# The first stage of a spectral layer and a gated feed-forward network, dealt out anew over the engines of one core

## The chip, the core and the metric

The kernel runs on one core of a Trainium2 chip. The core has engines with a queue of their own each: PE (TensorE, matmuls; its weight loads are listed as PEld), DVE (VectorE), ACT (ScalarE), POOL (GpSimd) and SP (SyncE, which here only issues transfers). Transfers are carried by 16 DMA engines. An engine works through its instructions in program order and waits on semaphores for what others produce. The metric is the device time of one execution in microseconds (us).

## The reference

`x` has 2048 rows of 576 elements (bf16). A global spectral filter is added to it, then a gated feed-forward network with 4608 hidden columns:

```
X = rfft2(layernorm(x))               # over rows and columns, 2048 x 289
y = irfft2(X * (w_r + 1j * w_i))      # bf16
h = x + y
n = layernorm(h)
out = h + (gelu(n @ w_gate) * (n @ w_up)) @ w_down
```

## The kernel before

The whole transform is done with matmuls against tables of sines and cosines that the kernel makes itself. `h_sb` holds the 2048 rows as 16 groups of 128 (one row group h is `h_sb[:, h, :]`). The order of every engine's instructions is that of the program text: `tc.manual_schedule()` is set, so nothing is moved by a planner.

**First stage.** Constants are written by DVE (`zerob` and others, L78 to L87). POOL writes the index ramps (`iota`, L173, called from L181 on) and the identity matrix; DVE makes from them the angles `mu` (L202), the mask (L212), `s2p` and `ks` (L217, L219). The row statistics of `x` come in two ways: even groups, and 13 and 15, by DVE (`sd`, which calls `ln_dve`, L117 to L119, three instructions), the other odd ones by ACT (`ln_act`, L124, two passes with a sum each, completed on POOL by `ln_fin`, L128 and L129). POOL turns variances into reciprocal roots four or two groups at a time (`ln_rstd`, L133 and L134, the second a power). `norms(lo, hi)` normalises groups on DVE (`xn`, L137) and calls `row16(h)` for each: PE multiplies the group by the row table `F16` (L306; remainder columns by `row16_rest`, L319). `fill` (L294) issues matmuls whose result nobody reads: 16 before the first group, 1 before each of groups 1 to 11, 5 behind the last. ACT brings the products from PSUM to `Bt` (`evict`, L330, and `evict4`, L336; the last `evict4` is DVE's).

Beside it tables are made. `DT` holds the column sines: the turns `kd` (`turns`, L271 and L272), the phases `pd` (`phases`, L276) and an operation that drops the sign (`drop_sign`, L225) on DVE, then two passes on ACT (`col_sin`, L355). `DF`, `DI` and `DS` hold shifted parts of `DT`: `DF` by two DVE copies (L414, L415), `DI` by one transfer and one DVE copy (L444), `DS` by four transfers (`sine_rows`, L431). `TF` holds the twiddle factors, 9 slices: angles on DVE (`angle_a`, L238 and L246; `angle_b`, L249 and L225), `sine` and `cosine` on ACT (L253, L256), `minus_sine` on DVE (L259), and `turn_tf` (L262), a transposing transfer to `TI`. Two slices (`first`) are made at the start and seven (`rest`) later. The spectral weights `WR` and `WI` come by transfers (L154), their far rows through two indirect transfers issued by POOL (L376, `wm_r` and `wm_i`) and one DVE operation each (L434, L436); two short DVE operations halve the edge columns (L438).

All PSUM tiles of this part come from one ring of four buffers (`two`, L66), so a product can start only when the tile four allocations back has been evicted.

**Second stage.** The loop from L651 on runs over eight pairs of row frequencies (`order`). For each pair: `f2` (L483, six matmuls with `Bt` against `DT` and `DF`; evicted to `pq` by ACT, one of them by DVE, L491), `f3` (L498, L499, twiddle matmuls with `TF`; evicted by ACT, L519), `sums_of` (L528, L529, DVE), `wmul` (L546 to L558, the spectral weights on DVE; the sums of the next pair are made in its middle), `i3` (L574, L576, matmuls with `TI`). In its first rounds the loop also makes the `rest` of the twiddles and calls `late_tables` (L444 to L456: the `DI` copy, four matmuls into `pt`, two ACT passes to `G16`).

**Third part.** Column products back (`inv_cols`, L623), the sum with `x` (`add_rows`, `add_sum`), the second layer norm, and the feed-forward network: 4 blocks of 512 rows, 36 hidden tiles each (`gu`, L881), then `acc` (L901). Its weights come in groups of three tiles (`load_gu`, L145, two transfers of 432 KB); the first three groups are called for at L155, ahead of the first stage's work, and `wd_a` (1728 KB) behind `turn_tf(rest)`. SP issues all transfers but POOL's two, in program order.

Of the kernel before, what the change touches and what calls it, by code (L numbers as in the profile page):

```python
# [10 lines left out]
ALU = mybir.AluOpType  # L11
# [30 lines left out]
def kernel_body(  # L42
# [129 lines left out]
    def iota(t, pattern, base=0, cm=0):  # L172
        G.iota(t, pattern=pattern, base=base, channel_multiplier=cm, allow_small_or_imprecise_dtypes=True)  # L173
# [23 lines left out]
    iota(iJ[:], [[1, 2], [2, JH]])  # L197
    rev = tmp("rev", [P, 1])
    iota(rev[:], [[0, 1]], 2 * P - 1, -2)

# [9 lines left out]
    V.tensor_scalar(iu[:], iu[:], 7, None, op0=ALU.bitwise_and)  # L210
    mask = tmp("mask", [P, P], FP32)
    V.tensor_scalar(mask[:], iu[:].rearrange("p c l -> p (c l)"), 0.0, None, op0=ALU.is_equal)  # L212
# [8 lines left out]
    iDs = tmp("iDs", [P, 3], FP32)  # L221
# [26 lines left out]
    def angle_b(sl):  # L248
# [12 lines left out]
    def turn_tf(sl):  # L261
        nc.sync.dma_start(  # L262
            TI[:, sl].rearrange("p k r q -> p (k r) q"), TF[:, sl].rearrange("p k r q -> p (k r q)"), transpose=True
        )

    pd, kd = tmp("pd", [P, 3, JP], FP32), tmp("kd", [P, 3, JP], FP32)
    C23 = 8388608.0

    def turns():
        for t in range(3):  # L270
            V.tensor_scalar(kd[:, t, :], iJ[:], iDs[:, t : t + 1], C23, op0=ALU.mult, op1=ALU.add)  # L271
        V.tensor_scalar(kd[:], kd[:], -C23, -float(D), op0=ALU.add, op1=ALU.mult)  # L272

    def phases():
        for t in range(3):
# [20 lines left out]
    def row16(h):  # L296
        if h % 2 == 0 or h == H - 1:
            ps_f[h] = two("f2t")
        if h % 4 == 0:
            ps_f["f4", h] = two("f4")  # L300
        f2t, b = (ps_f[h], 0) if h in ps_f else (ps_f[h - 1], 1)
        fill(f2t[:, b, :], 16 if h == 0 else 1 if h < 12 else 0)
        x = xn[:, h, :]
        for t in range(2):
            for n, d0 in ((0, t * P), (1, DH + t * P)):
                T.matmul(  # L306
                    f2t[:, b, t * 2 * P : (t + 1) * 2 * P],
                    lhsT=x[:, d0 : d0 + P],
                    rhs=F16[:, n : n + 2, :],
                    start=(n == 0),  # L310
                    stop=(n == 1),
                )
        if h < 12:
            row16_rest(h)
# [46 lines left out]
        )  # L361

    first, rest = slice(0, 2), slice(2, 9)
    angle_a(first)
    angle_b(first)
    ln_act(1)
    ln_act(3)
    sine(first)
    cosine(first)
    sd(0)  # L370
    row_table()
    sd(2)
# [2 lines left out]
    for t, w in zip(wm, (A_w_r, A_w_i)):  # L375
# [6 lines left out]
    turns()  # L382
    minus_sine(first)
    turn_tf(first)
    ln_act(5)
    ln_act(7)
    norms(0, 4)
    sd(4, 6)
    ln_fin(slice(5, 8, 2))
    ln_rstd(rstd, mv, 4, 8)  # L390
    evict(0, 2)
    evict4(0)
    ln_act(9)
    phases()
    norms(4, 8)
    drop_sign(kd[:], pd[:])
    ln_act(11)
    evict(4, 6)
    evict4(4)
    col_sin(1, pd, zerob)  # L400
    sd(8, 10)
    ln_fin(slice(9, 12, 2))
    ln_rstd(rstd, mv, 8, 12)
    sd(12, 13)
    ln_rstd(rstd, mv, 12, 14)
    norms(8, 12)
    sd(14, 15)
    ln_rstd(rstd, mv, 14, 16)
    evict(8)
    col_sin(0, kd, hpib)  # L410
    evict(10)
    evict4(8)
    norms(12, 16)
    V.tensor_copy(DF[0:32], D3[0:32])  # L414
    V.tensor_copy(DF[96:128], D3[96:128])  # L415
    for h in range(12, 16):
        row16_rest(h)
    evict(12, 14, 15)
    fill(two("f2t")[:, 0, :], 5)

    def sine_rows():


        for dst, src in (
            (DI[64:128, :, 1, :], DT[0:64, 0, :, 1, :]),
            (DS[0:64, 0, :, :], DT[64:128, 0, :, 1, :]),
            (DS[64:128, 0, :, :], DT[0:64, 1, :, 1, :]),
            (DS[0:64, 1, :, :], DT[64:128, 1, :, 1, :]),
            (DS[64:128, 1, :, :], D3[0:64, :, 1, :]),
        ):  # L430
            nc.sync.dma_start(dst, src)  # L431

    def weights():
        V.tensor_copy(WR[:, 9 : H + 1, 0:J], wm[0][:].rearrange("p (r j) -> p r j", r=8))  # L434
        evict4(12)
# [4 lines left out]
    weights()  # L440
    sine_rows()

    def late_tables():
        V.tensor_copy(DI[0 : J - 2 * P, :, 0, :], D3[0 : J - 2 * P, :, 0, :])  # L444
        pt = two("pt")
        for x in range(2):
            for p0 in (0, 64):
                T.matmul(
                    pt[p0 : p0 + 64, 0, x * P : (x + 1) * P],
                    lhsT=F16[:, 0, 64 * x : 64 * x + 64],  # L450
                    rhs=ident[:],
                    start=True,
                    stop=True,
                )
        for sign in range(2):
            A.activation(  # L456
                G16[:, sign, :, :].rearrange("p x q -> p (x q)"),
                pt[:, 0, 0 : 2 * P],
                ACT.Copy,
                scale=G_SCALE if sign == 0 else -G_SCALE,  # L460
            )

    xn_pool.__exit__(None, None, None)
    spw = tc.tile_pool(name="spw", bufs=1)
# [13 lines left out]
    def f2(c):  # L478
        ps = two("pq_ps")
        col = slice(slot[c] * P, (slot[c] + 1) * P)  # L480
        for par in range(2):
            for t in (par, par + 2, 4):
                T.matmul(  # L483
                    ps[:, par, 0:JP],
                    lhsT=Bt[:, t, col],
                    rhs=DT[:, t // 2, par] if t < 4 else DF[:, par],
                    start=(t == par),
                    stop=(t == 4),
                )
        sb = wk.tile([P, 2, JP], BF16, name="pq", tag="pq", bufs=6)  # L490
        (V.tensor_copy if c == 9 else A.copy)(  # L491
            sb[:].rearrange("p r (j a) -> p r j a", a=2),
            ps[:, :, 0:JP].rearrange("p a (r j) -> p r j a", r=2),
        )
        pq[c] = sb
# [156 lines left out]
    for i in range(n + 1):  # L652
# [12 lines left out]
        if 1 <= i <= n:  # L665
            f3(order[i - 1], 1)
            if i == 1:
                sums_of(order[0])
                sine(rest)
                angle_b(rest)  # L670
            else:
                if i == 2:
                    cosine(rest)
                    minus_sine(rest)
                    turn_tf(rest)
                    nc.sync.dma_start(wd_a[:], wd_view[:, 0:NWA, :])
                wmul(order[i - 2], i - 1, order[i - 1])
        if i >= 3 and not last:
# [288 lines left out]
```

## Time and profile before

| what | value |
|---|---|
| median of 3 runs | 508.18 us (508.09 to 509.54) |
| the profiled execution | 508.19 us, span 506.4 us |
| granted clock of PE | 0.999 |

Busy time of each engine by stretch, from the table of windows of the trace:

| stretch, us | what runs there | PE | DVE | ACT | POOL | DMA GB/s |
|---|---|---|---|---|---|---|
| 0 to 10.6 | tables, first statistics | 4.99 | 8.93 | 7.80 | 4.36 | 292 |
| 10.6 to 29.0 | row products | 14.84 | 16.94 | 13.76 | 8.03 | 243 |
| 29.0 to 35.7 | first `f2`, `f3` | 6.34 | 5.55 | 4.93 | 0 | 58 |
| 35.7 to 63.8 | `wmul` of all pairs | 27.00 | 27.61 | 26.09 | 0 | 89 |
| 63.8 to 78.0 | back, sum, second norm | 13.30 | 9.24 | 11.41 | 2.14 | 173 |
| 78.0 to 506.4 | feed-forward network | 424.83 | 147.29 | 87.19 | 9.63 | 112 |

The span runs from the first instruction to the last; the time of an execution has 1.8 us more around it. In lines of the timeline the first two numbers are start and duration in us, then come the engine, the line of the kernel, the operation, the tile written and the tiles read with their shapes, the count, and in brackets how long the engine had been idle and who released it. In the chain of waits a line is one piece of the path that ended last: start, length, engine, tile, line. Instructions of one engine overlap a little, so a duration can reach past the next start.

### The profile page before, as it was taken

Reading aid. Unit: us, or ns where it says so; the run is one execution under the profiler, and the core shown is the slowest. Engines: PE = TensorE matmul, PEld = TensorE weight load, DVE = VectorE, ACT = ScalarE, POOL = GpSimd, SP = SyncE. Lnnn points to the kernel's source line nnn. Section 1 sums busy time; section 2 is a strip of 40 time slices with the busy share of each in tenths; the row PEclk is TensorE's granted clock in tenths of the full one; section 3 lists DMA queues with packets and bytes.
Section 4 is the critical chain, followed back from the end, with each engine's and each line's share of the span. In section 5 each row is a group of like instructions: output and inputs, shape, how many; then the busy total and the mean of one; then the engine's idle time right before and its main releaser. Section 6 shows DMA issues by size and latency. Waiting matters only on the chain.

```text
span 506.4 us, 9895 instructions
## 1 busy us (share of the span) xinstructions
PE 491.3 (97%) x4342; PEld 291.2 (57%) x4342; DVE 215.6 (43%) x436; ACT 151.2 (30%) x265; POOL 24.2 (5%) x64
## 2 busy tenths in 40 slices
PE   5799999999999999999999999999999999999997
PEld 2466775555557764444477744444577544444775
DVE  8989964789651015533310034333201233333001
ACT  6888984222330003232300023333200132323000
POOL 4400010111110000000000000000000000000000
PEclk9999999999999999999999999999999999999999
DMA  9977068779970019997720089987500588880000
GB/s 293 247 89 195 1 167 215 148 147 195 185 143 1 0 48 191 187 201 151 154 57 0 1 187 197 186 166 151 100 0 1 119 163 155 160 153 3 12 13 25
DMA packets 86988, 60.86 MB, mean 120 GB/s; under 512 B 22688, under 2 KB 85536, under 8 KB 86944
## 3 DMA queue, kind: packets, MB, share of 16 engines
q1 hardware_dynamic: 86656, 59.03, 59.2%
q0 software_dynamic: 288, 1.18, 0.8%
q8 instruction: 34, 0.56, 0.5%
q14 instruction: 10, 0.08, 0.1%
HBM read 52.65 MB, written 2.36 MB: 109 GB/s over the span
## 4 chain that ended last, share of the span: by engine, by line
PE 91%; DVE 5%; DMA 1%; ACT 1%; POOL 1%; issue 0%; POOLq 0%; DVEq 0%
PE gu L881 55%; PE acc L901 28%; PE pq_ps L483 2%; DMA wd<-in_B_w_down_dram 1%; PE cs_ps L623 1%; PE eo_ps L576 1%; PE f2t L306 1%; PE eo_ps L574 1%; DVE xn L137 1%; PE gh_ps L499 1%; ACT cwb L636 1%; DVE st L118 1%; PE y_ps L746 1%; DVE st L117 1%; PE gh_ps L498 1%; POOL rstd L134 0%
## 5 line engine op out<-in xcount | busy, mean ns | idle before, releaser
L881 PE MATMUL gu<-Bt,wgu 64*128 64x512 bf16 x2592 | 281.5, 376 | 0.8 <-ACT cwb L636 0.8
L881 PEld LDWEIGHTS <-wgu 64*128 64x128 bf16 x2592 | 131.2, 94 | 147.9 <-issue 1.8
L889 ACT ACTIVATE g_sb<-gu 128x512 f32<-128x512 f32 x144 | 86.0, 597 | 302.7 <-PE gu L881 302.7
L890 DVE TENSOR_TENSOR P_sb<-g_sb,gu 128x512 bf16<-128x512 f32 x144 | 98.7, 685 | 152.8 <-ACT g_sb L889 152.8
L901 PEld LDWEIGHTS <-P_sb 128*128 128x128 bf16 x1152 | 112.4, 98 | 30.6 <-issue 2.4
L901 PE MATMUL acc<-wd,P_sb 128*128 128x288 bf16 x768 | 99.3, 286 | 0.0
L913 DVE TENSOR_TENSOR h_sb<-h_sb,acc 128x576 bf16<-128x576 bf16 x15 | 11.3, 754 | 118.2 <-PE acc L901 118.2
L901 PE MATMUL acc<-wd_a,P_sb 128*128 128x288 bf16 x384 | 52.3, 286 | 0.5 <-DVE h_sb L909 0.5
L294 PE MATMUL f2t<-h_sb,ident 128*128 128x512 bf16 x32 | 10.5, 434 | 4.4 <-DMA h_sb<-in_A_x_dram 4.4
L306 PE MATMUL f2t<-F,xn 128*128 128x256 bf16 x64 | 9.3, 273 | 4.8 <-DVE xn L137 4.8
L483 PE MATMUL pq_ps<-DT,Bt 128*128 128x290 bf16 x64 | 12.4, 287 | 0.0
L771 DVE TENSOR_SCALAR hrow<-h_sb,mv,rstd 128x1152 bf16<-128x1152 bf16 x14 | 12.1, 867 | 0.0
L134 POOL TENSOR_TENSOR rstd<-rstd,mhalf 128x1 f32<-128x1 f32 (+2 forms) x17 | 11.8, 692 | 1.4
L623 PEld LDWEIGHTS <-EO 128*128 128x128 bf16 x96 | 9.1, 96 | 3.0 <-issue 0.2
L483 PEld LDWEIGHTS <-Bt 128*128 128x128 bf16 x96 | 9.2, 97 | 2.5 <-ACT Bt L330 0.2
L491 ACT CAST pq<-pq_ps 128x580 bf16<-128x580 f32 x15 | 9.8, 667 | 1.9 <-PE pq_ps L483 1.9
L306 PEld LDWEIGHTS <-xn 128*128 128x128 bf16 x64 | 5.9, 98 | 7.7 <-DVE xn L137 6.1
L118 DVE BATCH_NORM_STATS2 st<-h_sb 128x6 f32<-128x288 bf16 x22 | 9.7, 442 | 0.0
L117 DVE BATCH_NORM_STATS2 st<-h_sb 128x6 f32<-128x288 bf16 x22 | 9.7, 442 | 0.0
L133 POOL TENSOR_SCALAR rstd<-mv 128x1 f32<-128x1 f32 (+2 forms) x17 | 4.3, 251 | 112.6 <-DVE mv L119 112.6
L330 ACT CAST Bt<-f2t 128x1024 bf16<-128x1024 f32 (+1 forms) x9 | 8.1, 927 | 5.0 <-PE f2t L306 5.0
L498 PE MATMUL gh_ps<-pq,TF 128*128 128x289 bf16 x32 | 8.7, 286 | 0.6 <-ACT TF L256 0.6
(134 smaller groups left out, 250.5 us busy)
## 6 DMA issues: line engine op xcount, KB each, us to landing
wgu<-in_B_w_gate_dram SPq DMA_DIRECT2D x48, 432.0 KB, 5.3
wgu<-in_B_w_up_dram SPq DMA_DIRECT2D x48, 432.0 KB, 6.7
wd<-in_B_w_down_dram SPq DMA_DIRECT2D x2, 1728.0 KB, 8.3
wd_a<-in_B_w_down_dram SPq DMA_DIRECT2D x1, 1728.0 KB, 8.4
out_dram<-h_sb SPq DMA_DIRECT2D x3, 576.0 KB, 3.3
h_sb<-in_A_x_dram SPq DMA_DIRECT2D x4, 288.0 KB, 3.3
h_sb<-in_A_x_dram SPq DMA_DIRECT2D x2, 576.0 KB, 5.6
WR<-in_A_w_r_dram SPq DMA_DIRECT2D x1, 650.2 KB, 7.8
```

The costliest lines, as they stand in the source:

```text
L117: V.bn_stats(st[:, 0, :], h_sb[:, h, 0:DH])
L118: V.bn_stats(st[:, 1, :], h_sb[:, h, DH:D])
L134: G.tensor_tensor(dst[:, sl], dst[:, sl], mhalf[:, sl], ALU.pow)
L306: T.matmul(f2t[:, b, t * 2 * P : (t + 1) * 2 * P], lhsT=x[:, d0 : d0 + P], rhs=F16[:, n : n + 2, :], start=(n == 0), stop=(n == 1),)
L483: T.matmul(ps[:, par, 0:JP], lhsT=Bt[:, t, col], rhs=DT[:, t // 2, par] if t < 4 else DF[:, par], start=(t == par), stop=(t == 4),)
L498: T.matmul(dst, lhsT=TF[:, ts[k1], t0, :], rhs=a, start=True, stop=False)
L623: T.matmul(ps[:, e, 0:JP], lhsT=EO[x][:, 2 * e + jt if jt < 2 else 4, 2 * g : 2 * g + 2].rearrange("p h e k l -> p (h e k l)"), rhs=DI[:, ...
L771: V.tensor_scalar(hrow[:], h_sb[:, h, :].rearrange("p (r k) -> p r k", k=64).unsqueeze(2).to_broadcast([P, NR, 2, 64]), mv2[:, h, 0:1], rs ...
L881: T.matmul(gu[:, c, :], lhsT=w[rows, r, i * P : (i + 1) * P], rhs=hl[tcnk % 2][rows, r, :], start=(r == 0), stop=(r == NR - 1),)
L889: A.activation(g_sb[:], gu[:, 0, :], ACT.Gelu_apprx_tanh)
L890: V.tensor_tensor(p_sb(fa + i), g_sb[:], gu[:, 1, :], ALU.mult)
L901: T.matmul(acc[:, c, 0:DH], lhsT=p_sb(f)[:, st * P : (st + 1) * P], rhs=wd[f // NWA][:, f % NWA, cc], start=(f == 0), stop=(f == NFT - 1),)
```

## The change

What moves to POOL: the memsets of `DF`, `DI` and the three `Zt` tiles (issued behind the reciprocal roots of groups 4 to 7); the scaling `iDs`; the turns `kd` (four operations, right behind the ramps). The addition of 192 to half of a column of `iD` becomes a second ramp over these partitions.

What moves to transfers on SP: the two `DF` copies, the `DI` copy, and the far rows of `WR`. All of SP's table transfers now stand in one row behind `norms(12, 16)`: the `WR` rows, `turn_tf(first)`, two into `DF`, two into `DI`, four into `DS`.

What changes place: the angles of the `first` twiddles go from ahead of the statistics to behind the statistics of group 6, and their sines behind the first evictions; statistics of group 4 go ahead of the first `norms`, and the rest of them are spread anew; `phases` and the sign operation go behind `norms(4, 8)`; `col_sin(0)` goes ahead of `evict(8)`. The `rest` of the twiddles: `angle_a`, `angle_b` and `sine` go between the row products and the first `f2`, with `late_tables`' matmuls and `G16`; a new `angle_c` (the sign), `minus_sine` and `weights` go behind the first two `f2`. Ahead of the first row group there are 10 fills instead of 16, ahead of `f2` 3 instead of 5. The first `f2` does its two products with `DF` last. The first three groups of feed-forward weights are called for behind `turn_tf(rest)`, ahead of `wd_a`.

The diff, cut to its core:

```diff
-    pre = [load_gu(g) for g in range(3)]
...
-    V.memset(DF[:], 0.0)
-    V.memset(DI[:], 0.0)
-    for z in Zts:
-        V.memset(z[:, :, J:], 0.0)
...
+    iota(iD[64:128, 2:3], [[0, 1]], 2 * P + 64 + 192, 1)
...
+    G.tensor_scalar(iDs[:], iD[:], 1.0 / D, None, op0=ALU.mult)
+    pd, kd = tmp("pd", [P, 3, JP], FP32), tmp("kd", [P, 3, JP], FP32)
+    C23 = 8388608.0
+    for t in range(3):
+        G.tensor_scalar(kd[:, t, :], iJ[:], iDs[:, t : t + 1], C23, op0=ALU.mult, op1=ALU.add)
+    G.tensor_scalar(kd[:], kd[:], -C23, -float(D), op0=ALU.add, op1=ALU.mult)
...
-    V.tensor_scalar(iD[64:128, 2:3], iD[64:128, 2:3], 192.0, None, op0=ALU.add)
-    V.tensor_scalar(iDs[:], iD[:], 1.0 / D, None, op0=ALU.mult)
...
+    def angle_b(sl):
         V.tensor_scalar(pr[:, sl], pr[:, sl], 2047, None, op0=ALU.bitwise_and)
         V.tensor_scalar(ab[:, sl], pr[:, sl], -1024.0, None, op0=ALU.add)
+
+    def angle_c(sl):
         drop_sign(ab[:, sl], ab[:, sl])
...
-        fill(f2t[:, b, :], 16 if h == 0 else 1 if h < 12 else 0)
+        fill(f2t[:, b, :], 10 if h == 0 else 1 if h < 12 else 0)
```

The order of the first stage after the change, from `first, rest = slice(0, 2), slice(2, 9)` on (V is DVE, A is ACT, G is POOL; `sd`, `norms`, angles and phases issue on DVE, `ln_act`, `evict`, `sine`, `cosine` and `col_sin` on ACT, `ln_fin` and `ln_rstd` on POOL):

```
ln_act(1); ln_act(3); sd(0); row_table(); sd(2)
ln_fin(1, 3); ln_rstd(rstd, mv, 0, 4); two indirect transfers on POOL
sd(4); ln_act(5); ln_act(7); norms(0, 4); evict(0, 2); evict4(0)
sd(6); ln_fin(5, 7); ln_rstd(rstd, mv, 4, 8)
G.memset(DF); G.memset(DI); G.memset of three Zt
angle_a(first); angle_b(first); angle_c(first); sine(first); cosine(first)
norms(4, 8); ln_act(9); ln_act(11); phases(); drop_sign(kd, pd)
sd(8); minus_sine(first); sd(10); ln_fin(9, 11); ln_rstd(rstd, mv, 8, 12)
evict(4, 6); evict4(4); col_sin(1, pd, zerob); col_sin(0, kd, hpib)
sd(12); norms(8, 12); sd(13); ln_rstd(rstd, mv, 12, 14)
sd(14, 15); ln_rstd(rstd, mv, 14, 16); evict(8, 10); evict4(8)
norms(12, 16)
SP: WR rows; turn_tf(first); DF, DF, DI, DI, DS x4
row16_rest(12..15); evict(12, 14, 15); angle_a(rest); evict4(12); angle_b(rest)
pt: 4 matmuls; G16: 2 ACT passes; sine(rest); fill(pt, 3)
```

And in the loop of the second stage:

```diff
         if i == 0:
             f2(order[0] + 8)
-            angle_a(rest)
+            angle_c(rest)
+            minus_sine(rest)
+            weights()
...
                 sums_of(order[0])
-                sine(rest)
-                angle_b(rest)
...
                     cosine(rest)
-                    minus_sine(rest)
                     turn_tf(rest)
+                    pre = [load_gu(g) for g in range(3)]
                     nc.sync.dma_start(wd_a[:], wd_view[:, 0:NWA, :])
...
-            late_tables()
```

More of the change, by code (lines that the diff above doesn't have):

```diff
@@ L195, in kernel_body @@
     iota(iD[:], [[P, 3]], 0, 1)
+    iota(iD[64:128, 2:3], [[0, 1]], 2 * P + 64 + 192, 1)
     iJ = tmp("iJ", [P, JP], FP32)
     iota(iJ[:], [[1, 2], [2, JH]])
+    iDs = tmp("iDs", [P, 3], FP32)
+    G.tensor_scalar(iDs[:], iD[:], 1.0 / D, None, op0=ALU.mult)
[4 more added lines that the diff above has]
+    G.tensor_scalar(kd[:], kd[:], -C23, -float(D), op0=ALU.add, op1=ALU.mult)
     rev = tmp("rev", [P, 1])
@@ L209, in kernel_body @@
     )
-    V.tensor_scalar(iu[:], iu[:], 7, None, op0=ALU.bitwise_and)
-    mask = tmp("mask", [P, P], FP32)
-    V.tensor_scalar(mask[:], iu[:].rearrange("p c l -> p (c l)"), 0.0, None, op0=ALU.is_equal)
     ia, s2a, s2p = tmp("ia", [P, 1]), tmp("s2a", [P, 1], FP32), tmp("s2p", [P, 1], FP32)
@@ L219, in kernel_body @@
     V.tensor_scalar(ks[:], kv[:], s2p[:, 0:1], None, op0=ALU.mult)
-    V.tensor_scalar(iD[64:128, 2:3], iD[64:128, 2:3], 192.0, None, op0=ALU.add)
-    iDs = tmp("iDs", [P, 3], FP32)
-    V.tensor_scalar(iDs[:], iD[:], 1.0 / D, None, op0=ALU.mult)
+    V.tensor_scalar(iu[:], iu[:], 7, None, op0=ALU.bitwise_and)
+    mask = tmp("mask", [P, P], FP32)
+    V.tensor_scalar(mask[:], iu[:].rearrange("p c l -> p (c l)"), 0.0, None, op0=ALU.is_equal)
     def drop_sign(dst, src):
@@ L245, in angle_a @@
         )
+    def angle_b(sl):
         V.tensor_scalar(pr[:, sl], pr[:, sl], 2047, None, op0=ALU.bitwise_and)
-    def angle_b(sl):
         V.tensor_scalar(ab[:, sl], pr[:, sl], -1024.0, None, op0=ALU.add)
+    def angle_c(sl):
         drop_sign(ab[:, sl], ab[:, sl])
@@ L264, in turn_tf @@
         )
[L266 to L272, printed above, removed]
     def phases():
@@ L363, in kernel_body @@
     first, rest = slice(0, 2), slice(2, 9)
-    angle_a(first)
-    angle_b(first)
     ln_act(1)
     ln_act(3)
-    sine(first)
-    cosine(first)
     sd(0)
@@ L381, in kernel_body @@
         )
-    turns()
-    minus_sine(first)
-    turn_tf(first)
+    sd(4)
     ln_act(5)
@@ L387, in kernel_body @@
     norms(0, 4)
-    sd(4, 6)
+    evict(0, 2)
+    evict4(0)
+    sd(6)
     ln_fin(slice(5, 8, 2))
     ln_rstd(rstd, mv, 4, 8)
-    evict(0, 2)
-    evict4(0)
+    G.memset(DF[:], 0.0)
+    G.memset(DI[:], 0.0)
+    for z in Zts:
+        G.memset(z[:, :, J:], 0.0)
+    angle_a(first)
+    angle_b(first)
+    angle_c(first)
+    sine(first)
+    cosine(first)
+    norms(4, 8)
     ln_act(9)
+    ln_act(11)
     phases()
-    norms(4, 8)
     drop_sign(kd[:], pd[:])
-    ln_act(11)
+    sd(8)
+    minus_sine(first)
+    sd(10)
+    ln_fin(slice(9, 12, 2))
+    ln_rstd(rstd, mv, 8, 12)
     evict(4, 6)
@@ L400, in kernel_body @@
     col_sin(1, pd, zerob)
[L401 to L404, printed above, removed]
+    col_sin(0, kd, hpib)
+    sd(12)
+    norms(8, 12)
+    sd(13)
     ln_rstd(rstd, mv, 12, 14)
-    norms(8, 12)
     sd(14, 15)
     ln_rstd(rstd, mv, 14, 16)
-    evict(8)
-    col_sin(0, kd, hpib)
-    evict(10)
+    evict(8, 10)
     evict4(8)
     norms(12, 16)
-    V.tensor_copy(DF[0:32], D3[0:32])
-    V.tensor_copy(DF[96:128], D3[96:128])
+    nc.sync.dma_start(WR[:, 9 : H + 1, 0:J], wm[0][:].rearrange("p (r j) -> p r j", r=8))
+    turn_tf(first)
+    for dst, src in (
+        (DF[0:32], D3[0:32]),
+        (DF[96:128], D3[96:128]),
+        (DI[64:128, :, 1, :], DT[0:64, 0, :, 1, :]),
+        (DI[0 : J - 2 * P, :, 0, :], D3[0 : J - 2 * P, :, 0, :]),
+        (DS[0:64, 0, :, :], DT[64:128, 0, :, 1, :]),
+        (DS[64:128, 0, :, :], DT[0:64, 1, :, 1, :]),
+        (DS[0:64, 1, :, :], DT[64:128, 1, :, 1, :]),
+        (DS[64:128, 1, :, :], D3[0:64, :, 1, :]),
+    ):
+        nc.sync.dma_start(dst, src)
     for h in range(12, 16):
@@ L418, in kernel_body @@
     evict(12, 14, 15)
[L419 to L431, printed above, removed]
+    angle_a(rest)
+    evict4(12)
+    angle_b(rest)
+    pt = two("pt")
+    for x in range(2):
+        for p0 in (0, 64):
+            T.matmul(
+                pt[p0 : p0 + 64, 0, x * P : (x + 1) * P],
+                lhsT=F16[:, 0, 64 * x : 64 * x + 64],
+                rhs=ident[:],
+                start=True,
+                stop=True,
+            )
+    for sign in range(2):
+        A.activation(
+            G16[:, sign, :, :].rearrange("p x q -> p (x q)"),
+            pt[:, 0, 0 : 2 * P],
+            ACT.Copy,
+            scale=G_SCALE if sign == 0 else -G_SCALE,
+        )
+    sine(rest)
+    fill(pt[:, 1, :], 3)
     def weights():
-        V.tensor_copy(WR[:, 9 : H + 1, 0:J], wm[0][:].rearrange("p (r j) -> p r j", r=8))
-        evict4(12)
         V.tensor_scalar(WI[:, 9 : H + 1, 0:J], wm[1][:].rearrange("p (r j) -> p r j", r=8), -1.0, None, op0=ALU.mult)
@@ L438, in weights @@
             V.tensor_scalar(w[:, :, 0 : J : J - 1], w[:, :, 0 : J : J - 1], 0.5, None, op0=ALU.mult)
[L440 to L461, printed above, removed]
     xn_pool.__exit__(None, None, None)
@@ L480, in f2 @@
         col = slice(slot[c] * P, (slot[c] + 1) * P)
[L481 to L489, printed above, removed]
+        steps = [(par, t) for par in range(2) for t in (par, par + 2, 4)]
+        if c == order[0]:
+            steps.sort(key=lambda s: s[1] == 4)
+        for par, t in steps:
+            T.matmul(
+                ps[:, par, 0:JP],
+                lhsT=Bt[:, t, col],
+                rhs=DT[:, t // 2, par] if t < 4 else DF[:, par],
+                start=(t == par),
+                stop=(t == 4),
+            )
         sb = wk.tile([P, 2, JP], BF16, name="pq", tag="pq", bufs=6)
```

## The prediction

> **What bounds the kernel now.** I first read busy time and the 40 slices.
>
> ```profile
> PE 491.3 (97%) x4342; PEld 291.2 (57%) x4342; DVE 215.6 (43%) x436; ACT 151.2 (30%) x265; POOL 24.2 (5%) x64
> ...
> PE   5799999999999999999999999999999999999997
> ...
> DVE  8989964789651015533310034333201233333001
> ```
>
> PE is nearly full over the span, but DVE is near full in the first five slices (63 us), where the whole change lies. From 78 us on the feed-forward matmuls run back to back and can only be shifted. So I read the chain of waits for the head (start us, us, what):
>
> ```profile
> 10.61 1.65 DVE xn L137 x4
> ...
> 15.92 1.45 DVE xn L137 x4
> ...
> 21.63 0.31 DVE xn L137
> 21.99 0.61 PE f2t L306 x4
> ...
> 29.15 2.24 PE pq_ps L483 x18
> 31.41 0.64 ACT pq L491
> ...
> 33.27 0.47 DVE xab L528
> ...
> 35.77 1.35 DVE m L546 x2
> ```
>
> DVE sets the time to row 8 (21.55), PE's rows and the evictions up to `f2` (28.98), then ACT and DVE up to the first `wmul`. The timeline of DVE shows what follows:
>
> ```profile
> 39.38 0.76 DVE L546 TENSOR_TENSOR m<-xab,WR 128x1156 bf16<-128x1156 bf16 x1
> ...
> 43.07 0.76 DVE L546 TENSOR_TENSOR m<-xab,WR 128x1156 bf16<-128x1156 bf16 x1
> ...
> 46.77 0.76 DVE L546 TENSOR_TENSOR m<-xab,WR 128x1156 bf16<-128x1156 bf16 x1
> ```
>
> From 35.69 to 63.8 each `wmul` takes 3.70 us and DVE never idles. **The start of the first wmul, 35.69, sets the end**; the sum is the move of this one point.
>
> **The change, step by step.** Distances between starts are from the timelines of before; I place the new order with them.
>
> Start: the memsets of `DF`, `DI`, `Zts` (1.09 to 2.57 on DVE) leave, so `mu` waits for Pool's `ic` (1.10+0.56) and starts at 1.72. From `mu` to the first statistics were 3.76 us; `iD`, `iDs` and the first angles (4.69 to 6.33, 1.64) leave, so `sd(0)` is at 3.84 (its rows are there: ACT read them at 3.81). Then 0.98 to `row_table`, 0.51 to `sd(2)`, 0.97 to its end, 6.30. Now ACT is last: its sums for row 3 end at 6.57 as before, Pool's `mv` at 6.91, and scale and power (9.04 to 10.57, 1.53) bring **xn0 to 8.56 instead of 10.61**.
>
> Rows 4 to 7: Pool's own queue decides. Power end to next square was 2.86 (two indirect loads), 0.28 to `mv`, 0.27 to the scale, 1.56 to the power's end: 10.61-0.04-2.05=8.52, then 13.49, **xn4 at 13.53 instead of 15.92**. `sd(6)` is over at 8.56+1.57+0.97=11.10; the first angles (1.37) fill the hole that is left.
>
> Rows 8 to 11: the phases (1.33) had such a hole and now stand behind `norms(4, 8)`: 13.53+1.36+1.33+0.52 (sign)+0.97+0.21+0.97=18.89, then 1.60 for the reciprocal root: **xn8 at 20.53 instead of 21.55**. `sd(12)` lies in that wait.
>
> Rows 12 to 15: `sd(13)` was also under that wait and now comes behind `norms(8, 12)`: 20.53+1.31+0.97+1.90=24.71 for xn12 (24.76 before), +1.32=26.03 for xn14 (26.08). The gain is nearly gone: three statistics are left between two groups of rows. PE: row 14 starts 0.44 behind xn14, 26.47, row 15 ends 27.45, the remainders at 27.81 (27.91). ACT gains more, since `col_sin(0)` is now ahead of `evict(8)`: its last eviction ends at 28.2 (28.83). `evict4(12)` on DVE, queued behind `angle_a(rest)` (26.72+1.17=27.89), waits for PE anyway and ends at 28.6. Four `pt` matmuls and 3 fills (5 took 1.07) give 27.81+0.25+0.65: **f2 at 28.75 instead of 28.98**.
>
> To `wmul`: `f2` to the first `sums_of` took 4.29, so 33.04. In that stretch DVE has the eviction of pq9 to 31.12, sign 0.54, `minus_sine` 0.33, `WI` 0.67 and edges 0.34, ending at 33.00: just covered. `sine(rest)`, ahead of pq1 on ACT, ends near 30.1 and holds pq1 to 30.7; pq9 is later still (31.1), so it is free. After the sums (0.75) the 1.67 us of angle, sign, `DI` copy and `minus_sine` (34.02 to 35.69) are gone: **wmul at 33.79 instead of 35.69, gain 1.90**. Next, row pair 2 is needed at 33.79+2.2=36.0 and ACT has it at about 35.4; pair 3 at 39.7 against 39.2. So the 3.70 pace holds.
>
> Transfers. WR's far rows (0.77 on DVE) and `DF` (0.60) become transfers, as does a `DI` copy. SP now passes through the WR copy (waits for `wm_r`, under 20; its rows are touched only at 32.7), the first transpose (waits for `minus_sine`, 17.9), two `DF`, two `DI`, four `DS`. `col_sin(0)` ends on ACT near 21.6; at 0.6 per issue and some 2 us to land, `DF` is there at 25 to 26 against 29.25 (its products come last in the first `f2`). The six `wgu` loads (2.65 MB) go behind the second transpose, about 39 us; with `wd_a` 4.4 MB at 200 GB/s (the first 30 us moved 233 to 290) take 22 us, to 61, and the first is needed at 76: nothing. If that cover went, the first `gu` would wait by as much. A load beside the `wmul` pace (wd_a, 41 to 49) left it at 3.70.
>
> Unknown, Pool's `kd` (3 of 128x290, 1 of 128x870), which no row shows. Nearest:
>
> ```profile
> 2.74 0.41 POOL L173 IOTA iJ<- 128x290 f32 x1
> 2.86 0.33 DVE L203 TENSOR_SCALAR mu<-mu 128x32 int32<-128x32 int32 x1
> ...
> 9.71 0.61 DVE L272 TENSOR_SCALAR kd<-kd 128x870 f32<-128x870 f32 x1
> ```
>
> At the iota's pace they take 3x0.41+1.03, with `iDs` and gaps 2.8 us from 3.28: done at 6.1, and Pool's square isn't due until 6.44: nothing. An iota only writes; at twice the pace the end is 8.5, 2.2 late, and all of it reaches `f2`. I take the iota's pace, the same engine and width. Pool's memsets (13.5 to 15.3 by the same pace) end before the next square (17.4): nothing, unless they hold DVE: bounds 0 to 1.6, below.
>
> Sum: profiled execution 508.19 (span 506.4 and 1.8 around it; median 508.18) less 1.90: **506.3 us**.
>
> **Rivals.**
>
> 1. *Pool's streams hold DVE a little*: for it, the 32-wide operation above took 0.33 beside Pool's iota, a 128-wide one alone 0.22, and one `xn` took 0.62 instead of 0.42 beside the indirect load. Against it, DVE's 0.61 at 9.71 was not stretched beside Pool's power (9.51 to 10.57). If `row_table`, due at 5.3, waits for the long `kd` (to 6.2) 0.4 is lost, and one memset ahead of an `xn` costs 0.6: 507.3. [...]
>
> 2. *Other side: Pool is slow and holds DVE throughout.* `kd` at twice the iota's pace to 8.5, with `row_table` held, puts xn0 2.8 late; five memsets alternating with xn4 to xn7 add 1.6. 506.3+4.4=510.7. It decides from 1.9 us of delay on. Against it, DVE's first 3 us ran beside Pool with little stretch.
>
> 3. *PE falls to its slow pace.* Row 7 ends at 17.75, row 8 begins at 20.97: 3.2 us idle, where the longest gap before is 2.2. At the start seven fills were 0.42 apart for 2.9 us, then 0.22. If that comes back, rows 8 to 11 lose 1.45, of which 0.66 is slack before xn12: 507.1. [...]
>
> 4. *DF is late.* The first transpose's issue took 5.41 us and landed after 12.2, DS 6.1. With these, `DF` lands at 17.95+5.41+1.2+6.2=30.8, 1.5 late: 507.8. Against it, that queue was then full of `wgu`, and the second transpose, three times as large, took
>
> ```profile
> 20.48 5.41 SPq L262 DMA_TRANSPOSE TI<-TF  x1
> ...
> 37.90 3.15 SPq L262 DMA_TRANSPOSE TI<-TF  x1
> ```
>
> **Chances.** Forecast 0.48 (own range 505.7 to 506.9), rival 1 0.24, rival 2 0.15, rival 3 0.07, rival 4 0.04, better than the sum 0.02. About 0.3% (1.5 us) is what a measurement can tell from no change: under 506.7 is faster, over 509.7 slower. Faster: most of the forecast, a little of rival 1 and the last, 0.50; slower: rival 2 and some combinations, 0.17; else 0.33. Range 505.4 to 508.9: it takes in rivals 1, 3, 4 and the lower half of Pool's bounds, and leaves out rival 2.
>
> **What would show it.** xn0 near 8.6, xn4 13.5, xn8 20.5, xn14 26.0, `f2` 28.75, first `wmul` 33.8, steps of 3.70 behind it, first `gu` near 76. `kd` on Pool at 0.4 and 1.0 us each; `row_table` and `xn` at their old durations. It is wrong if xn0 is past 9.5, if xn4 to xn7 are spread over more than 1.5 us, if fills in rows 8 to 11 lie 0.4 apart, or if the pace after `wmul` is over 3.70.

## The result and the profile after

| | before | after | ratio |
|---|---|---|---|
| median, 20 runs each | 509.47 us (507.99 to 509.82) | 510.27 us (509.17 to 511.53) | 1.0024, interval 1.0013 to 1.0035 |
| the profiled execution | 508.19 us, span 506.4 | 510.21 us, span 508.3 | |
| its granted clock of PE | 0.999 | 0.993 | |

The changed kernel is 0.24% slower, and not 1.90 us faster as forecast. Both kernels show their times at several heights. In before the height goes with the granted clock: near 508.2 us the clock is 0.999 to 1.000, near 509.6 it is 0.996 to 0.997. In after it doesn't go with it so simply: near 509.2 stand five runs at 0.992 to 0.996, near 510.3 and 511.4 thirteen runs, nearly all at 0.992 to 0.993, and twice the time is 509.4 with the clock at 1.000. How much of the difference between the medians is a matter of the clock has to be separated by the experiments.

The page of after: busy time, and the 40 slices with the granted clock (9 is 90% or more).

```profile
PE 493.3 (97%) x4334; PEld 291.7 (57%) x4334; DVE 212.7 (42%) x421; ACT 151.6 (30%) x265; POOL 28.4 (6%) x75
...
PE   6799999999999999999999999999999999999996
...
DVE  7879974689662015433311034433201233333001
...
PEclk9899999999999999999999999999999999999999
```

DVE was relieved of 2.9 us (215.6 to 212.7), POOL has 4.2 us more. PE has 2.0 us more with eight matmuls fewer: it worked more slowly somewhere, and the clock row has an 8 in the second slice, 12.7 to 25.4 us.

The chain of waits of after (start us, us, what), to be laid beside that of before:

```profile
13.65 2.63 DVE xn L137 x4
...
21.80 0.44 DVE xn L137
...
24.55 0.85 PE f2t L298 x4
...
26.18 0.87 PE f2t L298 x4
27.05 0.02 issue
27.07 1.01 ACT Bt L322
...
30.47 0.57 ACT G L443 x2
31.05 0.04 issue
31.09 0.81 PE pt L286 x3
31.89 2.24 PE pq_ps L479 x18
...
36.02 0.47 DVE xab L524
...
36.89 1.45 DVE m L542 x2
```

Three things are new. The four `xn` of rows 4 to 7 take 2.63 us where they took 1.45. Four row products of rows 10 and 11 take 0.85 and more where four took 0.61. And ahead of `f2` stands a link that the prediction doesn't have: the three fills into `pt`, which it counts by their length alone, wait for ACT's `G` passes. The first `wmul`, the point on which the sum was built, starts at 36.89 instead of 35.69; the forecast was 33.79.

**POOL's memsets and the rows.** Timelines of after, DVE's rows and then POOL's queue:

```profile
8.63 1.45 DVE L137 TENSOR_SCALAR xn<-h_sb,mv,rstd 128x576 bf16<-128x576 bf16 x4 [1.10 <-POOL rstd L134]
13.65 2.63 DVE L137 TENSOR_SCALAR xn<-h_sb,mv,rstd 128x576 bf16<-128x576 bf16 x4 [1.27 <-POOL rstd L134]
21.80 1.45 DVE L137 TENSOR_SCALAR xn<-h_sb,mv,rstd 128x576 bf16<-128x576 bf16 x4 [0.63 <-POOL rstd L134]
```

```profile
13.57 0.57 POOL L379 MEMSET DF<- 128x580 bf16 x1
14.10 0.57 POOL L380 MEMSET DI<- 128x580 bf16 x1
14.62 0.48 POOL L382 MEMSET Zt<- 128x124 bf16 x3
```

The same instruction, four times: 1.45 us without a memset beside it, 2.63 with the five memsets beside it, which take 1.6 us themselves. Cut to narrower windows, the same timeline shows the first and the second of the four alone:

```profile
13.65 1.61 DVE L137 TENSOR_SCALAR xn<-h_sb,mv,rstd 128x576 bf16<-128x576 bf16 x1 [1.27 <-POOL rstd L134]
...
15.18 0.41 DVE L137 TENSOR_SCALAR xn<-h_sb,mv,rstd 128x576 bf16<-128x576 bf16 x1
```

So the four are not slowed evenly: the first ends at 15.26, just behind POOL's last memset (15.09), and the others take 0.41 to 0.42 us as they do elsewhere. Everything up to here is as forecast within 0.12 us (xn0 8.63 against 8.56, xn4 13.65 against 13.53); from here on it is 1.2 late.

**The fills.** PE's timeline of after, ahead of `f2`; the bracket gives how long PE had been idle and who released it:

```profile
29.54 0.30 PE L435 MATMUL pt<-ident,F 128*64 128x128 bf16 x4
31.09 0.81 PE L286 MATMUL pt<-h_sb,ident 128*128 128x512 bf16 x3 [1.24 <-ACT G L443]
```

The fills write the other half of the tile whose first half ACT has to read for `G16`. ACT comes to that at 30.32, behind its evictions, and PE stands for 1.24 us.

**The clock.** The windows of after: stretch, its length, busy time of PE, PEld, DVE, ACT and POOL with the number of instructions, then the granted clock, DMA share, GB/s.

```profile
13.60:17.00 3.40, 1.68 (x14) 0.96 (x15) 3.35 (x6) 3.40 (x9) 1.50 (x6) 1.00 0.67 261
17.00:20.40 3.40, 3.40 (x17) 1.48 (x15) 3.30 (x11) 2.32 (x6) 0.39 (x2) 0.52 0.46 142
20.40:23.80 3.40, 1.83 (x14) 0.87 (x13) 2.74 (x9) 2.93 (x4) 1.27 (x2) 0.98 0.31 60
23.80:27.20 3.40, 3.40 (x17) 1.49 (x16) 2.80 (x10) 1.14 (x2) 1.91 (x4) 0.52 0.17 38
```

Twice a stretch in which PE is busy for half the time (1.68 and 1.83 us of 3.40) is followed by one at half the clock (0.52). The edges of the cuts can be read off: windows of this trace laid at 17.13, 20.54, 23.96 and 27.37 us have the clock at exactly 0.50, 1.00 and 0.50, so in this execution it was switched in steps of 3.41 us. The hold on rows 4 to 7 makes the first hollow stretch (PE idle for 1.79 us); the wait for rows 8 makes the second (1.57 us).

### The profile page after: what moved, and what is told of

It reads as the page before. It is cut to its first block, busy times and chain, and to the rows that moved or that the text cites. A ratio compares the mean times of both kernels' runs of the same rounds, so it can differ in the third digit from the quotient of the medians.

```text
span 508.3 us, 9886 instructions
## 1 busy us (share of the span) xinstructions
PE 493.3 (97%) x4334; PEld 291.7 (57%) x4334; DVE 212.7 (42%) x421; ACT 151.6 (30%) x265; POOL 28.4 (6%) x75
## 4 chain that ended last, share of the span: by engine, by line
PE 91%; DVE 3%; POOL 2%; ACT 1%; issue 1%; DMA 1%; POOLq 0%
PE gu L877 55%; PE acc L897 28%; PE pq_ps L479 2%; PE cs_ps L619 1%; PE eo_ps L572 1%; PE y_ps L742 1%; PE eo_ps L570 1%; DMA Bt<-hrow 1%; PE gh_ps L495 1%; POOL rstd L134 1%; DVE xn L137 1%; ACT Bt L322 1%; DVE h_sb L787 1%; PE f2t L298 1%; PE gh_ps L494 1%
## 5 line engine op out<-in xcount | busy, mean ns | idle before, releaser
L298 PE MATMUL f2t<-F,xn 128*128 128x256 bf16 x64 | 11.5, 320 | 3.7 <-DVE xn L137 3.7
L619 PE MATMUL cs_ps<-DI,EO 128*128 128x290 bf16 x32 | 9.1, 285 | 0.0
```

The lines of the kernel that those rows point to most:

```text
L298: T.matmul(f2t[:, b, t * 2 * P : (t + 1) * 2 * P], lhsT=x[:, d0 : d0 + P], rhs=F16[:, n : n + 2, :], start=(n == 0), stop=(n == 1),)
L619: T.matmul(ps[:, e, 0:JP], lhsT=EO[x][:, 2 * e + jt if jt < 2 else 4, 2 * g : 2 * g + 2].rearrange("p h e k l -> p (h e k l)"), rhs=DI[:, ...
```

## Experiments

**Without the fills into `pt`.**

```diff
-    fill(pt[:, 1, :], 3)
```

> The changed kernel without the three fills into the second half of the pt tile. Theory (three waits took the gain: Pool's memsets hold DVE 1.2 us, the fills wait for ACT's two G16 passes 1.2 us, PE at half clock some 0.8 us): f2 starts when the last eviction is done, near 30.5 instead of 31.73, first wmul 35.7 instead of 36.89, time 1.2 us below the changed kernel. Rival (the fills are covered, f2 waits for the evictions or its DF rows anyway): f2 stays at 31.7 and the time within 0.3 us.

Measured: 508.17 us median (507.96 to 509.97), ratio to before 0.9990 (0.9979 to 1.0002). The wait for `G` is gone and `f2` starts 0.55 us behind the `pt` matmuls, at 29.55; the first `wmul` is at 34.87. Both are some 0.9 us earlier than expected. The clock is as low as in after (0.993), but in this execution it is at half from 14.74 to 21.57 us, in rows 4 to 7, and not in rows 10 and 11; `xn` of row 8 starts at 21.79 as in after, PE still waits 0.40 us for it, and the time, 508.06, is near the lowest of this kernel (507.96, with the clock at 0.997). So what a cut cost depended on where it fell: here that wait was left over, in after the cuts put `f2` off by 0.94 us (worked out below). Leaving the fills out is worth 1.2 us between the lowest times (509.17 to 507.96) and 2.1 between the medians, the clock included; the rows 4 to 7 still take 2.62.

**The memsets on DVE, in holes of its queue.**

```diff
-    G.memset(DF[:], 0.0)
-    G.memset(DI[:], 0.0)
-    for z in Zts:
-        G.memset(z[:, :, J:], 0.0)
...
     sd(4)
+    V.memset(DF[:], 0.0)
...
     angle_c(first)
+    V.memset(DI[:], 0.0)
+    for z in Zts:
+        V.memset(z[:, :, J:], 0.0)
```

> The changed kernel with the memsets of DF, DI and Zt back on DVE, in its two idle holes (behind the statistics of group 4 and behind the first angles). Theory: the four xn of groups 4 to 7 take 1.36 to 1.45 us again instead of 2.63, xn8 at 20.5 instead of 21.80, f2 near 30.5, time 1.2 us below the changed kernel, but for what the clock does. Rival (xn was stretched by its own reads or by transfers, not by Pool): xn4 to xn7 still spread over 2.6 us, time the same or up to 0.3 us longer.

Measured: 509.04 us (508.82 to 510.11), ratio 1.0004 (0.9993 to 1.0015). Rows 4 to 7 are back at 1.45, and row 8 starts at 20.59 instead of 21.80. Against after that is 1.23 us between the medians, but 0.35 between the lowest times, and none of the twelve runs has a clock over 0.997. The windows of this execution show where it is lost:

```profile
17.00:20.40 3.40, 1.03 (x7) 0.43 (x6) 2.87 (x11) 3.40 (x6) 1.42 (x4) 1.00 0.78 209
20.40:23.80 3.40, 2.72 (x14) 1.26 (x15) 3.14 (x10) 1.49 (x3) 0.78 (x3) 0.64 0.09 22
```

With the rows on time PE ends row 7 earlier and then idles 3.05 us until row 8, and the clock is cut behind that, so that rows 8 to 10 take longer (0.79, 1.06 and 0.95 us for four products, 0.60 in row 11). In this trace the cut runs from 21.37 to 24.79, and the 3.41 us ahead of it hold the whole gap:

```profile
17.96:21.37 3.41, 0.36 (x4) 0.27 (x4) 2.72 (x11) 3.41 (x5) 1.27 (x2) 1.00 0.51 124
21.37:24.79 3.42, 3.42 (x17) 1.46 (x15) 3.32 (x12) 1.28 (x2) 0.94 (x2) 0.50 0.17 38
```

**Both.**

> Both: no fills into pt, memsets on DVE. Theory: the two waits add up, f2 near 29.3, first wmul 34.5 to 34.9 instead of 36.89 (before 35.69), time 2.2 to 2.4 us below the changed kernel and 0.8 to 1.2 below the kernel before, with a spread from the clock left. Rival (the waits cover each other, or PE at half clock was the whole loss): not more than 1.2 us below the changed kernel, no faster than before.

Measured: 507.90 us (506.90 to 508.99), ratio 0.9983 (0.9972 to 0.9993). The twelve runs stand at three heights: one at 506.90 with the clock at 0.999, six near 507.8 at 0.996 to 0.997, five near 508.9 at 0.993. The profiled execution is the one at 506.90, and it has the same stretch with the same work as the experiment ahead:

```profile
17.00:20.40 3.40, 1.03 (x7) 0.43 (x6) 2.87 (x11) 3.40 (x6) 1.48 (x4) 1.00 0.86 231
20.40:23.80 3.40, 2.72 (x21) 1.56 (x22) 3.14 (x10) 2.32 (x3) 0.78 (x3) 1.00 0.10 24
```

PE busy 1.03 us of 3.40 in both; then a cut in one (0.64) and none in the other (1.00). So a hollow stretch makes a cut possible and not certain. What differs is where the clock's steps of 3.41 us lie. By the trace's record of the clock it came up to full speed at 7.72 us in the experiment ahead, where the cut falls four steps behind that (21.37), and at 10.30 in after, where the first cut falls two steps behind (17.13). Here it came up at 9.27. Counted on in steps of 3.41, which is an estimate from those two executions, since this one has no cut in these rows to show an edge, an edge here falls at 19.50, in the middle of the gap, and splits it:

```profile
16.09:19.50 3.41, 1.78 (x14) 0.92 (x13) 3.31 (x11) 3.41 (x9) 0.62 (x3) 1.00 0.59 180
19.50:22.92 3.42, 1.84 (x14) 1.05 (x15) 2.73 (x9) 2.46 (x4) 1.04 (x1) 1.00 0.28 55
```

That fits these two executions, but it doesn't give the limit: in after two steps with PE busy 1.81 and 1.84 us were followed by a cut, and here 1.78 and 1.84 were not. In this kernel the heights go with the clock, and from one to the next it is 0.9 to 1.1 us (506.9, 507.8, 508.9). That this is the cost of one cut is an estimate: 3.41 us at half the clock take 0.0034 off its mean over a span of 505.1 us, and the heights lie 0.002 to 0.004 apart in it.

**The kernel before with the clock kept up.**

```diff
-        fill(f2t[:, b, :], 16 if h == 0 else 1 if h < 12 else 0)
+        fill(f2t[:, b, :], {0: 20, 4: 4, 8: 6}.get(h, 1 if h < 12 else 0))
```

> The kernel before with more fills ahead of groups 0, 4 and 8 (20, 4 and 6 instead of 16, 1 and 1), in PE's idle time before these groups. Theory (PE's clock is cut to a half for about 3.4 us after a stretch of 3.4 us in which PE was idle for half of it; the two heights of the kernel before, 508.2 and 509.6, are executions without and with such a cut): all executions near 508.2, none near 509.6, median about 0.7 us below that of before. Rival (the two heights come from elsewhere, the last output transfers for example): both heights stay.

Measured: 508.20 us (508.12 to 508.33), clock 1.000 in all twelve runs; ratio 0.9985 (0.9976 to 0.9995). Of the 35 runs of before on the same chip 21 stood at 509.5 to 509.8. The longer fills remove that height and change nothing below it, so **508.20 is what before costs with the clock left out**.

**The changed kernel with the clock kept up** (fills of 10, 4 and 11 ahead of rows 0, 4 and 8).

> The changed kernel with more fills ahead of groups 4 and 8 (4 and 11 instead of 1 and 1), nothing else. Theory: the cuts of the clock go and with them the upper heights (510.3, 511.4); all executions near 509.2 with the two other waits in place, xn4 to xn7 over 2.6 us, fills into pt behind G16; still 1.0 us above the lower height of before. Rival (the cuts are the whole loss): 507 or less.

Measured: 509.16 us (508.99 to 509.40), clock 0.999 to 1.000; ratio to before as it is 1.0002 (0.9992 to 1.0012). Beside 508.20 that is a loss of 0.96 us that the clock has no part in; with 510.27 for after, the cuts are worth 1.1 us of its median. Its PE timeline still has the wait, and its windows have no cut:

```profile
29.99 0.81 PE L286 MATMUL pt<-h_sb,ident 128*128 128x512 bf16 x2 [0.83 <-ACT G L443]
```

```profile
17.00:20.40 3.40, 3.24 (x21) 1.72 (x21) 3.30 (x11) 3.17 (x6) 1.09 (x3) 1.00 0.57 174
```

**Both waits removed and the clock kept up** (the third experiment with the same fills of 10, 4 and 11).

> No fills into pt, memsets on DVE (as in e3), and more fills ahead of groups 4 and 8 (4 and 11 instead of 1 and 1). Theory (the heights of e3, 506.9, 507.8 and 508.9, are none, one and two cuts of PE's clock): all executions near 506.9, clock 1.0, f2 near 28.4, first wmul 33.7; 1.3 us below the lower height of the kernel before (508.2). Rival (the heights of e3 come from elsewhere, the second layer norm's transposes for example): three heights stay.

Measured: 506.92 us (506.86 to 506.93), ratio 0.9954 (0.9940 to 0.9968). Timelines of DVE and PE:

```profile
20.60 1.45 DVE L137 TENSOR_SCALAR xn<-h_sb,mv,rstd 128x576 bf16<-128x576 bf16 x4 [0.62 <-POOL rstd L134]
...
28.38 0.67 PE L478 MATMUL pq_ps<-DT,Bt 128*128 128x290 bf16 x4 [0.28 <-ACT Bt L322]
...
33.70 0.77 DVE L541 TENSOR_TENSOR m<-xab,WR 128x1156 bf16<-128x1156 bf16 x1
...
76.40 4.92 PE L876 MATMUL gu<-Bt,wgu 64*128 64x512 bf16 x44 [1.20 <-DMA Bt<-hrow]
```

The first `wmul` is at 33.70 where the prediction put it at 33.79. Against the changed kernel with the same fills that is 2.24 us, and nothing but the fills into `pt` and the memsets differs.

**The fills back, one step earlier.** The last kernel with the three fills ahead of the `pt` matmuls, where ACT has nothing to read yet:

```diff
     pt = two("pt")
+    fill(pt[:, 1, :], 3)
     for x in range(2):
```

> This is the kernel with the memsets on DVE, the fills into the pt tile left out and the row-0, row-4 and row-8 fills at 10, 4 and 11 (506.92 us, f2 at 28.38, first weight product at 33.70), with the same three filler products put back one step earlier, ahead of the transposes into the pt tile, where ACT has not yet been asked to read it. Theory (the three fillers cost 1.1 to 1.2 us because PE waits for ACT's read of the tile, not because of their own length): without that wait they cost their own time, some 0.4 us, or nothing where PE would have been idle: f2 at 28.4 to 28.9, time 506.9 to 507.4. Rival (the fillers themselves, or a third tile in use, cost it): f2 at 29.4 to 29.6, time 508.0 to 508.2.

Measured: 507.29 us (507.27 to 508.14), ratio 0.9973 (0.9961 to 0.9985). PE's timeline:

```profile
27.94 0.82 PE L286 MATMUL pt<-h_sb,ident 128*128 128x512 bf16 x3
28.69 0.30 PE L436 MATMUL pt<-ident,F 128*64 128x128 bf16 x4
28.92 0.67 PE L479 MATMUL pq_ps<-DT,Bt 128*128 128x290 bf16 x4
```

No bracket, so no wait: the fillers cost 0.37 us of time by their own length, as the theory expected. What they cost beyond that in the changed kernel is the wait behind ACT. One of the ten runs took 508.14 with the clock at 1.000, so there are heights that the clock doesn't make; what made this one isn't known.

**The memsets moved to another group of rows.** The changed kernel with POOL's memsets behind `ln_rstd(rstd, mv, 8, 12)`, and fills of 4 and 6 ahead of rows 4 and 8.

> The changed kernel with Pool's five memsets put behind the second group's reciprocal deviations instead of behind the first group's, and the fills ahead of rows 4 and 8 at 4 and 6. Theory (Pool's memset and DVE's normalised rows exclude each other, so the hold goes where the memsets go): the normalised rows 4 to 7 fall back from 2.63 to about 1.45 us and rows 8 to 11 rise from 1.36 to about 2.6 us; row 12 and everything behind it comes as late as in the changed kernel, 509.2 us within 0.4. Rival (rows 4 to 7 are slow for a reason of their own, such as their reads or the order on DVE): rows 4 to 7 stay near 2.6 us, or rows 8 to 11 stay near 1.4 us and the time falls by about 1 us to 508.2.

Measured: 509.99 us (508.87 to 510.32), ratio 1.0017 (1.0004 to 1.0029). The median misses the expected 509.2 within 0.4, since the fills of 4 and 6 didn't keep the clock up: the three runs with the clock at 1.000 took 508.87 to 509.25, as the changed kernel with the clock kept up, and seven at 0.995 to 0.997 took 509.9 to 510.3. The timelines of DVE and POOL:

```profile
13.65 1.45 DVE L137 TENSOR_SCALAR xn<-h_sb,mv,rstd 128x576 bf16<-128x576 bf16 x4 [1.27 <-POOL rstd L134]
...
20.63 2.33 DVE L137 TENSOR_SCALAR xn<-h_sb,mv,rstd 128x576 bf16<-128x576 bf16 x4 [0.62 <-POOL rstd L134]
```

```profile
20.55 0.58 POOL L394 MEMSET DF<- 128x580 bf16 x1
21.07 0.58 POOL L395 MEMSET DI<- 128x580 bf16 x1
21.59 0.84 POOL L397 MEMSET Zt<- 128x124 bf16 x3
```

The hold follows the memsets from one group to the next (2.33 for the expected 2.6; the first `xn` of row 8 takes 1.32, and POOL's last two memsets, which end behind it, 0.36 and 0.39 where such a one took 0.19), and row 12 comes nearly as late as in the changed kernel with the clock kept up (25.70 and 25.84). That rules out a cause that sits in rows 4 to 7.

**The late twiddle part alone**, put into the kernel before with the fills of 20, 4 and 6: `angle_a(rest)`, `evict4(12)`, `angle_b(rest)`, the `pt` matmuls, `G16` and `sine(rest)` ahead of the first `f2` in place of the five fills, `angle_c`, `minus_sine` and `weights` behind the first two; memsets, turns, transfers and loads as before.

> On the kernel before with its clock kept up (e4): the late twiddle angles, G16 and their place alone, without fills ahead of f2; memsets, turns, DF, DI and WR as before. Theory: DVE is done with DF at 27.4, angle 28.5, last eviction 29.2, so f2 at 29.2 (28.98); sums 4.3 behind that plus 0.7 for the WR copy that now lies there, wmul near 35.0 instead of 35.69: 0.6 to 0.7 us below 508.2. Rival (ACT, with sine ahead of the first pq, becomes the bound): first wmul at 35.7 or later, no gain.

Measured: 507.18 us (507.12 to 507.77), ratio 0.9961 (0.9947 to 0.9975); beside 508.20 a gain of 1.02, more than the expected 0.6 to 0.7. DVE's timeline shows the first `wmul` 1.05 us earlier:

```profile
34.49 0.22 DVE L688 COPY DI<-DT 33x290 bf16<-33x290 bf16 x1
34.64 0.75 DVE L547 TENSOR_TENSOR m<-xab,WR 128x1156 bf16<-128x1156 bf16 x1
```

One operation of the four that stood there is left. With 506.92 for the whole change without its waits, the new division of the first stage adds 0.26 us.

**The loads later alone**: in the kernel before with the fills of 20, 4 and 6, the first three `load_gu` behind `turn_tf(rest)`.

> On the kernel before with its clock kept up (e4): the first three groups of feed-forward weights called for behind the second transpose, nothing else. Theory: hidden in both places, 508.2, nothing beyond 0.1 us. Rival (the early loads hold up the table transfers or the later ones delay TI or the first gu): 0.3 us or more either way.

Measured: 508.27 us (508.21 to 508.36), beside 508.20 nothing; ratio 0.9983 (0.9974 to 0.9992), which is that of the fills. The first `wmul` stays at 35.69. In after, where the loads stand at the same place, the first transpose takes 1.32 us to issue, no longer behind them in SP's queue; in before it takes 5.41.

**A version beyond both.** The kernel of 506.92 us with row 9's statistics on ACT ahead of the evictions of rows 0 to 3, and row 13's on ACT instead of DVE:

```diff
     norms(0, 4)
+    ln_act(9)
     evict(0, 2)
...
-    ln_act(9)
...
-    evict(4, 6)
+    evict(4)
+    ln_act(13)
+    evict(6)
...
-    sd(13)
+    ln_fin(slice(13, 14))
```

> The kernel of 506.92 us with one further step: the statistics of row 9 on ACT ahead of the eviction of rows 0 to 3, and those of row 13 on ACT instead of DVE. Theory (ahead of the first f2 the chain still hangs on DVE's statistics and normalised rows): row 12's normalised rows about 0.9 us earlier, f2 at 27.5 to 27.9, first weight product near 33.0, and the time down by 0.2 to 0.7 us to 506.2 to 506.7, less than the gain at f2 because the first gate product waits for the second norm's rows. Rival (ACT's evictions then end the waits, and nothing is left on DVE): f2 within 0.2 of 28.38 or later, 506.9 or above.

Measured: 506.15 us (506.09 to 506.18), ratio 0.9950 (0.9931 to 0.9968). Timelines of DVE and PE:

```profile
23.89 0.72 DVE L137 TENSOR_SCALAR xn<-h_sb,mv,rstd 128x576 bf16<-128x576 bf16 x2
...
28.02 0.67 PE L480 MATMUL pq_ps<-DT,Bt 128*128 128x290 bf16 x4 [0.68 <-ACT Bt L322]
```

Row 12 is 0.90 earlier as expected, but `f2` only 0.36 (28.38 to 28.02, missing the expected 27.5 to 27.9): ACT's last eviction ends the wait now, as the rival said. So the theory is right up to row 12, and at `f2` the rival's mechanism takes over. But the time is 0.77 below 506.92, more than the gain at `f2`, where both expected less: the first `wmul` is 0.52 earlier (33.18) and the first `gu` 0.77 (75.63). Why the gain grows on the way isn't shown.

## Why the prediction was wrong, point by point

The steps of the sum, with the chip's numbers for the changed kernel, for it with the clock kept up, and for it without the two waits and with the clock kept up (starts in us, from the profiled executions):

| point | predicted | after | clock kept up | and both waits removed |
|---|---|---|---|---|
| `xn` of rows 4 to 7 | 13.53 | 13.65 | 13.50 | 13.63 |
| `xn` of rows 8 to 11 | 20.53 | 21.80 | 21.65 | 20.60 |
| `xn` of row 12 | 24.71 | 25.99 | 25.84 | 24.79 |
| first `f2` | 28.75 | 31.73 | 30.64 | 28.38 |
| first `wmul` | 33.79 | 36.89 | 35.79 | 33.70 |
| first `gu` | near 76 | 79.37 | 78.17 | 76.40 |
| time | 506.3 | 510.21 | 509.01 | 506.88 |

**What failed.**

1. *"Pool's memsets ... nothing, unless they hold DVE: bounds 0 to 1.6."* They held it. The term was 1.2 us, not 0: one `xn` waited behind the whole run of memsets. The row that the prediction weighed against a hold, DVE's 0.61 beside POOL's power at 9.71, was of a single kind of work; the rows to go by were the 32-wide operation and the one `xn` that it named itself. Rival 1 had the hold at half its size (0.6, one memset ahead of one `xn`, where five were ahead of it); rival 2 let five memsets alternate with the rows for 1.6, which didn't happen in after either. That the memsets are the cause is shown by the rows being back at 1.45 us with DVE writing the tiles, and by the hold that moved with the memsets (2.33); what makes the one engine wait for the other no run shows. In after the hold lasted for a run of five instructions and not for one.

2. *"Four `pt` matmuls and 3 fills ...: 27.81+0.25+0.65."* This counted the fills by their length and missed that they add a wait: they write a tile that ACT reads, and ACT stood behind its evictions. With the clock kept up PE waited 0.83 us, in the profiled execution of after 1.24. Their length is 0.37 us of time. No rival had this; the question that was left out is who else holds the tile that a filler writes.

3. *The clock.* The sum puts nothing for it; *rival 3, PE's slow pace, was given 0.07*, and that for a gap of 3.2 us ahead of row 8, with 2.2 as the longest of before (its trace has none over 1.71). In after PE was never idle for longer than 1.79 us in rows 4 to 11, and the clock was cut twice. Nor does the hold widen the gap ahead of row 8: 1.57 us in after, where the cut clock stretched rows 6 and 7 besides (1.06 us for four products, 0.60 in row 5), and 3.05 with the memsets on DVE. Comparing the profiled executions with and without the cuts, `f2` comes 1.09 later, of which 0.15 is there at row 8 already: 0.94 us.

For the profiled execution the first `wmul` is 3.10 late against the sum: 1.27 at row 8 (0.12 at row 4, the rest the memsets), 0.94 for the clock, 0.77 that is left up to `f2` (the wait behind `G`), and 0.12 between `f2` and `wmul`. Then 0.20 more up to the first `gu` (42.48 for before's 42.28), 0.50 between there and the end of the span, 0.12 around it: together 3.92 for the 3.91 between 506.3 and 510.21. Two small sums of the prediction don't close (27.81+0.25+0.65 is 28.71 and not 28.75; 8.5 is 2.1 and not 2.2 behind 6.44); nothing hangs on them.

**What held.** The early rows (8.63 and 13.65 for 8.56 and 13.53). `kd` on POOL at 1.70 for three, 0.5 to 0.7 each where 0.41 was taken, and 0.92 for the long one, over at 6.60 instead of 6.1, just ahead of POOL's next square at 6.67; the third short one, and not the long one of rival 1, stretched `row_table`'s second operation from 0.20 to 0.40. `DF` was in time: the first transpose took 1.32 us to issue on a queue without the weight loads in it, and SP went on to `DF` at 23.39, so rival 4 falls. The later loads cost nothing. The late part is worth 1.02 alone and the pace behind the first `wmul` stayed at 3.70. Without the two waits and the cuts the chain comes out at 33.70 for 33.79, so the frame of the sum was right and the terms above were not. The closeness is in part luck: that kernel has no fills ahead of `f2`, which the sum counts at 0.65, and with the fills back one step earlier the first `wmul` is at 34.09.

Rival 2's 510.7 lies near the measured time, but 2.8 us of it are `kd` at half its pace and rows 0 late, and neither happened; that it comes near is luck.

**What is left.** Even at 506.92 it misses 506.3. The gain is 1.99 at the first `wmul` but 1.57 at the first `gu`: the second norm's transposes are issued 1.97 us earlier (72.96 to 70.99), and the first `gu` starts 5.41 us behind that where it was 5.01, released by their landing and no longer by ACT. From there to the end of the span it is 428.7 where it was 428.4 (428.9 in after), though PE's and DVE's last work keeps its distance from the first `gu` within 0.02: the difference lies behind the last addition. What makes those transfers land later wasn't tried and stays open. Open too is how much of the clock's cuts in the changed kernel comes from the memsets: the hold makes one of the hollow stretches, but with the rows on time PE idles longer ahead of row 8 (3.05 us for 1.57) and was cut there as well.

## What to carry to other kernels

Before work is moved to an idle engine, look at what runs beside it at its new place: a run of memsets on POOL held one of DVE's normalised rows for 1.2 us, while the same memsets in holes of DVE's own queue left these rows on time. A filler matmul has a destination: here three of them stood 1.24 us behind ACT's read of the tile that they write, and cost 0.37 us when they were put ahead of that read and nothing when they were left out. Where the granted clock differs from execution to execution, compare kernels with the clock kept up in both: here the cuts made 1.1 us of the changed kernel's median, and the change itself, with the clock kept up, 0.96.

## What the runs showed that was not expected

In after the clock of PE was cut to half for 3.41 us, twice, behind stretches of 3.4 us in which PE was busy for 1.68 and 1.83 us and never idle for longer than 1.79. Nor does a hollow stretch always bring a cut: at 1.03 of 3.40 one execution had it and another, with the same instructions there, had not; in the one the gap lay within one step of the clock, in the other, by the count in steps of 3.41 us, across two. And a cut didn't always cost time: with the clock at half from 14.74 to 21.57 us the kernel without the fills into `pt` still waited 0.40 us for `xn` of row 8 and took 508.06, near its lowest (507.96). No limit can be read from these runs: idle gaps of 1.79 and 1.57 us were followed by a cut, and one of 3.05 was once and once not. The cuts come in steps of 3.41 us, and the clock came up to full speed at another point in each of these executions (7.72 and 9.27 us in the two above, 10.30 in after).
